# An FFT convolution on one Trainium2 core: the last two frequency slots contracted from copied lanes instead of from a DMA gather

## Chip, cores and metric

One core of a Trainium2 chip runs the whole program. The metric is the time of one execution on the device in microseconds (us), a median over runs; a profiled execution gives the trace. Engines are named as the profile names them: PE (TensorE matmul), PEld (its weight load), DVE (VectorE), ACT (ScalarE), POOL (GpSimd), SP (SyncE, which here only issues DMAs).

## What is computed

A 7x7 circular convolution of one 224x224 image with 96 channels in and 96 out, written with FFTs:

```python
wp = jnp.pad(w, ((0, H - K), (0, W - K), (0, 0), (0, 0)))
Xf = rfft2(x, axes=(1, 2)); Wf = rfft2(wp, axes=(0, 1))
Yf = jnp.einsum('bhwi,hwio->bhwo', Xf, Wf)
y = irfft2(Yf, (H, W), axes=(1, 2)).astype(jnp.bfloat16)
```

Inputs and output are bf16, x is 1x224x224x96 and w is 7x7x96x96.

## The kernel before

The kernel doesn't run two-dimensional FFTs. Along the height it cuts the image into 8 blocks of 28 rows (`NJ`, `B`) and takes a short real transform of each, as a matmul with a matrix `Fm`; that gives 17 frequency slots (`NS`) of two parts (real and imaginary; in the first and last slot two real values). Along the width it works in polyphase form with a fast three-term FIR scheme on the taps. The inverse transform along the height is again a matmul, with a matrix `G`.

The width is cut into 7 tiles `t` of 32 pixels; a tile is 16 pixel pairs `w` (`TW`). Work on a tile runs in 17 rounds, one per slot `s` (`b_round`, line 607). A round convolves over the width on PE into two PSUM banks, b0 and b1; between the two halves and behind the second the program calls `mid()` and `end()`, which put other PE work there. ACT multiplies b0 by -0.5 (`tt_`), which DVE's `u` and `v` read beside b0 and b1; their sum (`ysum`, on DVE or POOL) is the round's result `yf`, 128 partitions (16 w by 8 blocks) by 384 (two parts, two phases of a pixel pair, 96 channels). In the last tile, TL = 6, the sums of slots 14, 15 and 16 are on DVE. DVE also builds the planes `J` that PE convolves (`jit`, line 566).

Results are written to DRAM (`scr`) in groups of three slots, read back with partitions turned to (block, slot, part) and contracted by `G`: the jobs of `c_jobs` (line 776), eleven per tile, each two matmuls of 384 columns and two evictions. `CQ[6] = (3, 5)` puts eight jobs into the last tile's rounds; six jobs of tile 5 are left over when it ends. Rounds, jobs and everything else are in an order written out by hand: each engine's instructions are chained in program order (`_Ordered`, line 91), and the DMAs of SP form one queue, those of ACT another. `evac` and `tail_evac` (lines 132 and 142) choose DVE or ACT for each eviction from a running sum of modelled costs; `tail_evac` holds once `tail[0]` is set.

The last tile can't wait for a full round trip, so it is split by `SLAST = (0, 9, 12, 15, 17)`:

- Slots 0 to 8 are written to `scra`, read back in round 11 as `tl_a` (72 rows: 4 blocks x 9 slots x 2 parts, the other 4 blocks beside them), and contracted with `GA`, which holds four copies of `G`'s rows on its diagonal.
- Slots 9 to 11 and 12 to 14 go through `scrb` into 48 rows each of `tl_b` (`load_b`, line 753), the first in round 14, the second behind round 16.
- Slots 15 and 16 are turned on the core: a matmul with a permutation `PT` (`turn_mm`, line 720), a copy to SBUF (`turn_out`, line 725), and for each slot and part one DMA that takes 128 packets of 384 bytes into 8 rows of `tl_b`. Two of the four are issued by SP and two by ACT.
- `GB` (128 rows: 8 blocks x 8 slots x 2 parts) contracts `tl_b`, in two column sets for the two halves of the blocks.

Behind round 16 (lines 1013 to 1031) the six late jobs run, three before the turning matmuls and three after, then the queued output DMAs. The closing stage (lines 1036 to 1062) makes 16 output tiles of 112 x 384: `first` multiplies `tl_a` by `GA` into a PSUM bank, `second` adds `tl_b` by `GB` and evicts. Eight firsts run ahead (eight banks); ten matmuls on a zeroed tile `wu` (`WARM`) stand between them and the seconds, adding nothing to the sums; the other eight firsts are woven in from the fifth second on.

The matrices are made far ahead: `GA`, `GB` and `PT` are zeroed by POOL in round 15 of the first two tiles, which run woven together (lines 938 to 945), and filled by 28 small SP DMAs in tiles 3 and 4 (`g_parts`, line 756). The last tile-5 row group (`LATE`) is loaded in round 5 of tile 6 over filter slots 5 and 6, which are no longer needed then.

Of the kernel before, what the change touches and what calls it, by code (L numbers as in the profile page):

```python
# [14 lines left out]
B = 28  # L15
# [18 lines left out]
PGRP = ((0, 5), (5, 8), (8, 11), (11, 14), (14, 17))  # L34
YGRP = ((0, 3), (3, 6), (6, 9), (9, 12), (12, 15), (15, 17))
YGRPL = ((0, 3), (3, 6), (6, 9), (9, 12), (12, 15), (15, 17))
SLAST = (0, 9, 12, 15, 17)
SA = SLAST[1]
ND = SLAST[-2]
SLOAD = (SA + 2, 14)  # L40
YMAX = 3
YBUF = 4
JGB = ((0, 3), (3, 6), (6, 9), (9, 12), (12, 15), (15, 17))
# [23 lines left out]
def kernel(  # L67
# [92 lines left out]
    KA = 4 * 2 * SA  # L160
    NL = len(SLAST) - 1
    KB = [NJ * 2 * (SLAST[i + 1] - SLAST[i]) for i in range(1, NL)]
    RB = [sum(KB[:i]) for i in range(NL - 1)]
    assert sum(KB) == 128
# [550 lines left out]
    tt_tiles = {}  # L715
    puts = []
    turns = {}
    zt = [WF[:, i].rearrange("p t o -> p (t o)")[:, 0:4 * C] for i in range(NS - ND)]

    def turn_mm(s):  # L720
        pz = bank()[:, 0:4 * C]
        TE.matmul(pz, lhsT=PT[:], rhs=turns[s], start=True, stop=True)
        return pz

    def turn_out(s, pz, copy, eng):
        i, n = s - ND, 2 * (NS - ND)
        copy(out=zt[i], in_=pz)
        for r in range(2):
            p = RB[-1] + 2 * i + r
            eng.dma_start(out=tl_b[p:p + (NJ - 1) * n + 1:n].rearrange("p w e -> p (w e)"), in_=zt[i][:, r * 2 * C:(r + 1) * 2 * C])  # L730

    def load_t(t, gi, h):
        if (t, gi, h) == LATE:
            tt = WF[:, 5:7].rearrange("p s t o -> p (s t o)")[:, 0:8 * 2 * C].rearrange("p (w e) -> p w e", e=2 * C)
# [16 lines left out]
    tl_b = tl_all[:, 2 * TW2:3 * TW2].rearrange("p (w e) -> p w e", e=2 * C)  # L751

    def load_b(i):
        dma(tl_b[RB[i]:RB[i] + KB[i]], scr_tiles[(TL, 1 + i)].rearrange("w j s (r e) -> (j s r) w e", r=2))

    def g_parts():
        for j in range(4):
            dma(GA[j * 2 * SA:(j + 1) * 2 * SA, j * B:(j + 1) * B], G[0:2 * SA, 0:B])
            yield
        for j in range(NJ):  # L760
            for i in range(NL - 1):
                s, s1 = SLAST[i + 1:i + 3]
                n = 2 * (s1 - s)
                dma(GB[RB[i] + j * n:RB[i] + (j + 1) * n, j // 4, j % 4 * B:(j % 4 + 1) * B], G[2 * s:2 * s1, 0:B])
# [11 lines left out]
    def c_jobs(t):  # L776
        jobs = []
        w0 = t * 2 * TW
        for gi, h in LT if t < TL - 1 else LTL:
# [3 lines left out]
            def mk_(q, gi=gi, h=h, nq=nq, hold=hold):  # L783
                def put(j0, nj, px, npx, row, col):
                    yo = hold["yo"]

                    def go():
                        dma(out[0, j0 * B:(j0 + nj) * B, w0 + px:w0 + px + npx, :].rearrange("h w c -> h (w c)"),
                            yo[row:row + nj * B, col:col + npx * C])
                    if tail[0] or t == TL - 1 and gi != 2:  # L790
                        outs.append(go)
                    else:
                        go()

                def f():
                    if q % 2 == 0:
                        hold["yo"] = new_yo()
                    tt = tt_tiles[(t, gi, h)]
                    yo = hold["yo"]
                    nj = 2 if q == 2 else 3  # L800
                    for b in range(2):
                        pb = bank()[0:nj * B, 0:4 * C]
                        TE.matmul(pb, lhsT=G[0:nj * FR, 0:nj * B],
                                  rhs=tt[0:nj * FR, 4 * q + 2 * b:4 * q + 2 * b + 2, :].rearrange("p w e -> p (w e)"), start=True, stop=True)
                        k = 2 * (q % 2) + b
                        ev = (yo[0:nj * B, k * 4 * C:(k + 1) * 4 * C], pb, 4 * C)
                        if tail[0] == 2:
                            waiting.append(ev)
                        else:
                            evac(*ev)  # L810
# [17 lines left out]
    LATE = (TL - 1, 1, 1)  # L828
    LTL = ((2, 0), (0, 0), (1, 0), (0, 1), (1, 1))
    outs = []  # L830
    waiting = []
    NTT = 4
    held = [0, 0]
    pend = []
# [67 lines left out]
    for r in range(NS + LAG):  # L902
# [28 lines left out]
        if r == PGRP[-2][1] + 1:  # L931
# [7 lines left out]
            GB = g_pool.tile([128, 2, 4 * B], BF16, name="GB")  # L939
            GE.memset(GA[:], 0.0)  # L940
            GE.memset(GB[:], 0.0)
            PT = g_pool.tile([128, 128], BF16, name="PT")
            GE.memset(PT[:], 0.0)
            pv = PT.rearrange("p (j w) -> p j w", j=NJ)
# [16 lines left out]
    if NP2:  # L961
        ps0_cm.__exit__(None, None, None)
        ps_cms = [tc.tile_pool(name="ps", bufs=NP2, space=bass.MemoryType.PSUM),
                  tc.tile_pool(name="psb", bufs=8 - 2 * NP2, space=bass.MemoryType.PSUM)]
        pools["ps"], pools["psb"] = (c.__enter__() for c in ps_cms)
    cj = c_jobs(0)
    gp = g_parts()
    for t in range(2, NT):
        if t == TL:
            scr_tiles[t] = None  # L970
            scr_tiles[(t, 0)] = dr_pool.tile([TW, NJ, SA, 4 * C], BF16, name="scra")
            for i in range(1, NL - 1):
# [18 lines left out]
        for s in range(NS):  # L991
# [7 lines left out]
                queue_c(t - 1)  # L999
            if t in (3, 4):  # L1000
                next(gp, None)
            if t == TL and s == 5:
                load_t(*LATE)
            if t == TL and s in SLOAD:
                i = SLOAD.index(s)
                if i:
                    load_b(i - 1)
                else:
                    sv = scr_tiles[(TL, 0)].rearrange("w (g j) s (r e) -> (j s r) (w g) e", g=2, r=2)
                    for p0, p1 in ((0, 64), (64, KA)):  # L1010
                        dma(tl_a[p0:p1].rearrange("p w g e -> p (w g) e"), sv[p0:p1])
            b_round(t, s, fills(qs, 2 * s), fills(qs, 2 * s + 1), bool(now) if t < TL else s % 3 == 2 or s >= NS - 3, now)
    tail[0] = 1
    load["v"], load["a"] = 1000.0, 0.0
    cj.pop(0)()
    tail[0] = 2
    for _ in range(2):
        cj.pop(0)()
    tail[0] = 1
    pz = [turn_mm(s) for s in range(ND, NS)]  # L1020
    turn_out(NS - 1, pz[1], SE.copy, SE)
    turn_out(NS - 2, pz[0], VE.tensor_copy, DE)
    load_b(NL - 3)
    load["v"], load["a"] = 0.0, 1500.0
    for ev in waiting:
        evac(*ev)
    while cj:
        cj.pop(0)()
    assert not pend
    for f in outs:  # L1030
        f()
# [63 lines left out]
```

## Time and profile before

| what | value |
|---|---|
| median of three runs | 263.33 us (263.27 to 264.97) |
| profiled execution: time, span | 264.47 us, 262.8 us |
| mean granted PE clock | 0.985 |
| ACT, POOL busy | 197.3 us, 98.4 us |
| DVE's sum of slot 14, start and length | 242.31, 0.97 us |
| write of slots 12 to 14 issued (ACT) | 243.36 us |
| read of slots 12 to 14 issued (SP) | 248.47 us |
| turn DMAs issued: SP, ACT | 245.69 for 1.46 us, 245.99 for 1.96 us |

The span runs from the first to the last instruction; the profiled execution's own time is 1.67 us longer. Times inside the text are microseconds from the start of the span. Because every operation goes through the helper of `_Ordered`, nearly all instructions carry line 101, and they are told apart by engine, operation and tile. In the trace `xf` is also the memory of `tl_a` and `tl_b`, `J` and `yo` are the output buffers of the jobs, `xn` holds u and v of the last tile, and `tt` holds the last output tiles. A number in brackets behind an instruction is the idle time before it and what ended it.

### The profile page before, as it was taken

To read this page: it belongs to the slowest core of one execution; us is meant where nothing else is said; L and a number is where in the kernel's file an instruction comes from. 1 tells how busy PE (TensorE), PEld (TensorE's weight loads), DVE (VectorE), ACT (ScalarE), POOL (GpSimd) and SP (SyncE) were. 2 spreads that over 40 slices of the span, in tenths; PEclk is the share of its full clock that TensorE was granted. 3 is DMA by queue.
4 is the path that set the end of the run, shared out by engine and by line. 5 is a ranking of instruction groups with operands and counts; after the bars stand their busy time and mean duration, and the time that the engine had idled before them with its cause. 6 is when DMAs were issued, how large, how long until landed. Compare 5 with 4: busy or idle time off the path is not lost.

```text
span 262.8 us, 11954 instructions
## 1 busy us (share of the span) xinstructions
PE 252.9 (96%) x5040; PEld 233.1 (89%) x5040; DVE 221.7 (84%) x464; ACT 197.3 (75%) x470; POOL 98.4 (37%) x154
## 2 busy tenths in 40 slices
PE   8998999999999999999999999999999999989893
PEld 3988999999989999989999998999999999979472
DVE  6889898899999889868887888878988799999824
ACT  8889978697745967988988799887988852664423
POOL 7783124464657632232223412333134413225000
PEclk9999999999999999999999999999999999999869
DMA  6994104511111695997976596879958742878866
GB/s 185 270 184 128 47 6 147 166 50 47 47 51 47 197 258 91 289 331 198 273 209 209 143 283 196 207 203 266 285 158 194 251 136 87 213 188 237 201 210 203
DMA packets 46778, 46.58 MB, mean 177 GB/s; under 512 B 35324, under 2 KB 37952, under 8 KB 46724
## 3 DMA queue, kind: packets, MB, share of 16 engines
q1 hardware_dynamic: 45732, 44.24, 60.8%
q10 hardware_dynamic: 992, 1.57, 1.9%
q8 instruction: 39, 0.64, 1.1%
q14 instruction: 15, 0.12, 0.2%
HBM read 24.46 MB, written 21.14 MB: 174 GB/s over the span
## 4 chain that ended last, share of the span: by engine, by line
PE 71%; DVE 11%; DMA 6%; issue 5%; ACT 3%; POOL 2%; SPq 0%; DVEq 0%; POOLq 0%; ACTq 0%
PE pb L101 71%; DVE J L101 4%; DVE WF L101 3%; DMA WF<-in_x_dram 3%; DMA tt<-scr 2%; ACT xf L101 2%; POOL yf L101 2%; DMA wq<-in_w_dram 1%; DVE v L101 1%; DVE u L101 1%; ACT WF L101 1%; PE ps L101 1%; SPq L101 0%; DVE yf L101 0%; DVE tt L101 0%
## 5 line engine op out<-in xcount | busy, mean ns | idle before, releaser
L101 PE MATMUL pb<-WF,J 96*128 96x96 bf16 x2821 | 162.4, 206 | 1.8 <-DVE J L101 0.7
L101 PEld LDWEIGHTS <-J 96*128 96x128 bf16 x2821 | 137.9, 98 | 10.7 <-issue 3.6
L101 POOL TENSOR_TENSOR yf<-v,u 128x384 bf16<-128x384 f32 x70 | 73.0, 1056 | 124.0 <-issue 72.5
L101 ACT CAST xf<-pb 96x408 bf16<-96x408 f32 (+6 forms) x140 | 65.0, 489 | 3.7 <-PE pb L101 1.6
L101 PE MATMUL pb<-WF,xf 96*128 96x96 bf16 x952 | 59.9, 206 | 0.2
L101 DVE TENSOR_TENSOR J<-xf 96x456 bf16<-96x456 bf16 (+3 forms) x85 | 56.3, 701 | 0.0
L101 PEld LDWEIGHTS <-xf 96*128 96x128 bf16 x952 | 47.1, 98 | 1.0 <-PE ps L101 0.6
L101 PE MATMUL pb<-Fm,xn 118*128 118x136 bf16 (+4 forms) x576 | 43.9, 203 | 0.8 <-ACT WF L101 0.6
L101 PE MATMUL pb<-tt,Gm 102*84 102x384 bf16 (+1 forms) x128 | 31.4, 327 | 0.1
L101 ACT CAST yo<-pb 84x384 bf16<-84x384 f32 (+1 forms) x61 | 26.1, 480 | 5.6 <-PE pb L101 3.6
L101 PEld LDWEIGHTS <-xn 118*128 118x128 bf16 x576 | 28.6, 97 | 1.3 <-issue 1.1
L101 ACT CAST J<-pb 84x384 bf16<-84x384 f32 (+1 forms) x63 | 27.3, 490 | 2.1 <-DMA xf<-scrb 2.1
L101 DVE TENSOR_TENSOR J<-J 96x912 bf16<-96x912 bf16 (+2 forms) x42 | 25.3, 603 | 0.0
L101 ACT CAST WF<-pb 96x480 bf16<-96x480 f32 (+1 forms) x43 | 21.5, 556 | 0.9 <-PE pb L101 0.8
L101 PEld LDWEIGHTS <-wq 128*128 128x128 bf16 (+1 forms) x288 | 19.7, 149 | 0.2
L101 PE MATMUL pb<-wq 128*128 128x120 bf16 x192 | 15.2, 224 | 0.0
L101 DVE TENSOR_TENSOR WF<-WF 96x960 bf16<-96x960 bf16 x15 | 14.0, 934 | 1.4 <-ACT WF L101 1.3
L101 POOL TENSOR_TENSOR yf<-xn,xn 128x384 bf16<-128x384 f32 x9 | 8.8, 996 | 14.8 <-issue 12.1
L101 PEld LDWEIGHTS <-Gm 102*84 102x84 bf16 (+1 forms) x132 | 11.3, 117 | 1.6 <-issue 0.6
L101 DVE TENSOR_TENSOR yf<-v,u 128x384 bf16<-128x384 f32 x20 | 11.6, 578 | 0.7
L101 ACT COPY xf<-xf 96x816 bf16<-96x816 bf16 (+4 forms) x18 | 10.8, 652 | 0.0
L101 PEld LDWEIGHTS <-wu 128*128 128x128 bf16 (+1 forms) x33 | 4.8, 151 | 6.0 <-issue 2.9
(404 smaller groups left out, 270.8 us busy)
## 6 DMA issues: line engine op xcount, KB each, us to landing
scr<-yf SPq DMA_DIRECT2D x30, 288.0 KB
xn<-in_x_dram SPq DMA_DIRECT2D x12, 672.0 KB
tt<-scr SPq DMA_DIRECT2D x23, 336.0 KB
out_dram<-yo SPq DMA_DIRECT2D x12, 252.0 KB
out_dram<-J SPq DMA_DIRECT2D x12, 252.0 KB
tt<-scr SPq DMA_DIRECT2D x6, 288.0 KB
wq<-in_w_dram SPq DMA_DIRECT2D x5, 288.0 KB
WF<-in_x_dram SPq DMA_DIRECT2D x2, 672.0 KB
```

Source lines behind the costliest of these rows:

```text
L101: r = fn(*a, **k)
```

## The change

Slots 0 to 14 now all go through DRAM into `tl_a`, in three chunks (9, 3 and 3 slots), each chunk laid out as 4 blocks by slots by parts with the other four blocks beside them: 120 rows, and one pass with a larger `GA` contracts them. `tl_b`, `GB`, `PT` and the turn are gone.

Slots 15 and 16 aren't turned. Their result has (w, block) on its 128 partitions. For each of four pairs k of slot and part, four copies on DVE or ACT move 32 partitions (4 w by 8 blocks) of it to partitions 32k to 32k+31 of a tile `Z`, the four groups of w side by side. A contraction over the 128 partitions of `Z` picks one w and four blocks by its weights: `GZ` holds, for each of the 32 lanes, `G`'s row of the pair k where the lane matches and zero elsewhere. `GZ` is one POOL multiply of a mask `MK` (128x32) and `Gk` (G's rows spread over partitions by a small matmul with `SEL`), both broadcast to 128x32x28. `first` is now two matmuls of 192 columns with `GZ` (one per w), and `second` is the one with `GA`.

The six late jobs move between the last rounds: three behind round 14, one inside round 15, one behind it, one inside round 16 (`LATEJ`). The write of slots 12 to 14 is issued behind the first of them. `LATE` is loaded in round 3, over filter slots 2 and 3. The copies of slot 15 stand behind its round and the job there; those of slot 16 behind round 16, the last four on ACT, the other twelve on DVE. The read of slots 12 to 14 follows.

```diff
-SLAST = (0, 9, 12, 15, 17)
+SLAST = (0, 9, 12, 15)
-ND = SLAST[-2]
+ND = SLAST[-1]
+LATEJ = {29: 3, 30: 1, 31: 1, 32: 1}
...
+    def z_part(s, r, copy):
+        k = 2 * (s - ND) + r
+        for a in range(TW // 4):
+            zone = (k, a)
+            apart("Z", zone, copy(out=Z[k * QZ:(k + 1) * QZ, a], in_=turns[s][a * QZ:(a + 1) * QZ, r * 2 * C:(r + 1) * 2 * C]))
...
+    def load_a(i):
+        dma(tl_a[8 * SLAST[i]:8 * SLAST[i + 1]].rearrange("p w g e -> p (w g) e"),
+            scr_tiles[(TL, i)].rearrange("w (g j) s (r e) -> (j s r) (w g) e", g=2, r=2))
...
+    def g_turned():
+        pg = bank()[:, 0:B]
+        TE.matmul(pg, lhsT=SEL[0:FR], rhs=G[0:FR, 0:B], start=True, stop=True)
+        SE.copy(out=Gk[:], in_=pg)
+        GE.tensor_tensor(out=GZ[:], in0=MK.unsqueeze(2).to_broadcast([128, QZ, B]), in1=Gk.unsqueeze(1).to_broadcast([128, QZ, B]), op=ALU.mult)
...
-            GE.memset(GB[:], 0.0)
-            PT = g_pool.tile([128, 128], BF16, name="PT")
-            GE.memset(PT[:], 0.0)
-            GE.affine_select(out=pv, in_=pv, pattern=[[-1, NJ], [-NJ, TW]], compare_op=ALU.not_equal, fill=1.0, base=0, channel_multiplier=1)
+            GE.memset(MK[:], 0.0)
+            for k in range(NZ):
+                GE.affine_select(out=MK[:], in_=MK[:], pattern=[[-1, QZ]], compare_op=ALU.not_equal, fill=1.0, base=-k * QZ, channel_multiplier=1)
+            GE.memset(SEL[:], 0.0)
+            GE.affine_select(out=pv, in_=pv, pattern=[[-1, NZ], [0, QZ]], compare_op=ALU.not_equal, fill=1.0, base=-2 * ND, channel_multiplier=1)
...
+    g_turned()
     cj = c_jobs(0)
+    def last_jobs(k):
+        def f():
+            if not tail[0]:
+                tail[0] = 1
+                load["v"], load["a"] = 1000.0, 0.0
+            for _ in range(LATEJ.get(k, 0)):
+                cj.pop(0)()
+                if puts:
+                    puts.pop(0)()
+        return f
...
+            mid, end = fills(qs, 2 * s), fills(qs, 2 * s + 1)
+            if t == TL and s >= ND - 1:
+                mid, end = last_jobs(2 * s), lambda: None
+            b_round(t, s, mid, end, bool(now) if t < TL else s % 3 == 2 or s >= NS - 3, now)
+            if t == TL and s >= ND - 1:
+                last_jobs(2 * s + 1)()
+            if t == TL and s >= ND:
+                for r in range(2):
+                    z_part(s, r, SE.copy if s == NS - 1 and r else VE.tensor_copy)
+    load_a(NL - 1)
...
     def first(g, q):
         pc = bank()[0:M4, 0:4 * C]
-        TE.matmul(pc.rearrange("p (w e) -> p w e", w=2), lhsT=GA[:], rhs=tl_a[:, 2 * q:2 * q + 2, g], start=True, stop=False)
+        for i in range(2):
+            w = 2 * q + i
+            TE.matmul(pc[:, i * 2 * C:(i + 1) * 2 * C], lhsT=GZ[:, w % 4 * NJ + 4 * g:w % 4 * NJ + 4 * g + 4].rearrange("p j m -> p (j m)"),
+                      rhs=Z[:, w // 4], start=i == 0, stop=False)
         return pc
     def second(g, q, pc, yo):
-        TE.matmul(pc, lhsT=GB[:, g], rhs=tl_b[:, 2 * q:2 * q + 2, :].rearrange("p w e -> p (w e)"), start=False, stop=True)
+        TE.matmul(pc.rearrange("p (w e) -> p w e", w=2), lhsT=GA[:], rhs=tl_a[:, 2 * q:2 * q + 2, g], start=False, stop=True)
```

More of the change, by code (lines that the diff above doesn't have):

```diff
@@ L159 @@
     G = cpool.tile([3 * FR, 3 * B], BF16, name="Gm")
-    KA = 4 * 2 * SA
     NL = len(SLAST) - 1
-    KB = [NJ * 2 * (SLAST[i + 1] - SLAST[i]) for i in range(1, NL)]
-    RB = [sum(KB[:i]) for i in range(NL - 1)]
-    assert sum(KB) == 128
+    KA = 8 * ND
+    NZ = 2 * (NS - ND)
+    QZ = 128 // NZ
+    assert NZ == 4 and QZ == 4 * NJ
     XW = 2 * TW * C
@@ L717 @@
     turns = {}
[L718 to L730, printed above, removed]
+    def z_part(s, r, copy):
[3 more added lines that the diff above has]
+            apart("Z", zone, copy(out=Z[k * QZ:(k + 1) * QZ, a], in_=turns[s][a * QZ:(a + 1) * QZ, r * 2 * C:(r + 1) * 2 * C]))
     def load_t(t, gi, h):
         if (t, gi, h) == LATE:
-            tt = WF[:, 5:7].rearrange("p s t o -> p (s t o)")[:, 0:8 * 2 * C].rearrange("p (w e) -> p w e", e=2 * C)
+            tt = WF[:, 2:4].rearrange("p s t o -> p (s t o)")[:, 0:8 * 2 * C].rearrange("p (w e) -> p w e", e=2 * C)
         else:
@@ L750 @@
     tl_a = tl_all[0:KA, 0:2 * TW2].rearrange("p (w g e) -> p w g e", g=2, e=2 * C)
-    tl_b = tl_all[:, 2 * TW2:3 * TW2].rearrange("p (w e) -> p w e", e=2 * C)
-    def load_b(i):
-        dma(tl_b[RB[i]:RB[i] + KB[i]], scr_tiles[(TL, 1 + i)].rearrange("w j s (r e) -> (j s r) w e", r=2))
+    Z = tl_all[:, 2 * TW2:2 * TW2 + 8 * C].rearrange("p (a e) -> p a e", e=2 * C)
+    def load_a(i):
+        dma(tl_a[8 * SLAST[i]:8 * SLAST[i + 1]].rearrange("p w g e -> p (w g) e"),
+            scr_tiles[(TL, i)].rearrange("w (g j) s (r e) -> (j s r) (w g) e", g=2, r=2))
     def g_parts():
[L757 to L764, printed above, removed]
-                yield
+        for i in range(NL):
+            s, n = SLAST[i], 2 * (SLAST[i + 1] - SLAST[i])
+            for j in range(4):
+                p = 8 * s + j * n
+                dma(GA[p:p + n, j * B:(j + 1) * B], G[2 * s:2 * s + n, 0:B])
+                yield
+    def g_turned():
[3 more added lines that the diff above has]
+        GE.tensor_tensor(out=GZ[:], in0=MK.unsqueeze(2).to_broadcast([128, QZ, B]), in1=Gk.unsqueeze(1).to_broadcast([128, QZ, B]), op=ALU.mult)
     yo_free = [J_bufs[2][0:4 * B, i * PXC * C:(i + 1) * PXC * C] for i in range(2)]
@@ L806, in f @@
                         ev = (yo[0:nj * B, k * 4 * C:(k + 1) * 4 * C], pb, 4 * C)
[L807 to L810, printed above, removed]
+                        evac(*ev)
                     if q == 1 and gi < 2:
@@ L830 @@
     outs = []
-    waiting = []
     NTT = 4
@@ L938 @@
             GA = g_pool.tile([KA, 4 * B], BF16, name="GA")
-            GB = g_pool.tile([128, 2, 4 * B], BF16, name="GB")
             GE.memset(GA[:], 0.0)
-            GE.memset(GB[:], 0.0)
-            PT = g_pool.tile([128, 128], BF16, name="PT")
-            GE.memset(PT[:], 0.0)
-            pv = PT.rearrange("p (j w) -> p j w", j=NJ)
-            GE.affine_select(out=pv, in_=pv, pattern=[[-1, NJ], [-NJ, TW]], compare_op=ALU.not_equal, fill=1.0, base=0, channel_multiplier=1)
+            GZ = g_pool.tile([128, QZ, B], BF16, name="GZ")
+            Gk = g_pool.tile([128, B], BF16, name="Gk")
+            MK = g_pool.tile([128, QZ], BF16, name="MK")
+            SEL = g_pool.tile([128, 128], BF16, name="SEL")
+            GE.memset(MK[:], 0.0)
+            for k in range(NZ):
+                GE.affine_select(out=MK[:], in_=MK[:], pattern=[[-1, QZ]], compare_op=ALU.not_equal, fill=1.0, base=-k * QZ, channel_multiplier=1)
+            GE.memset(SEL[:], 0.0)
+            pv = SEL.rearrange("p (k q) -> p k q", q=QZ)
+            GE.affine_select(out=pv, in_=pv, pattern=[[-1, NZ], [0, QZ]], compare_op=ALU.not_equal, fill=1.0, base=-2 * ND, channel_multiplier=1)
         if r == 3:
@@ L971 @@
             scr_tiles[(t, 0)] = dr_pool.tile([TW, NJ, SA, 4 * C], BF16, name="scra")
-            for i in range(1, NL - 1):
+            for i in range(1, NL):
                 scr_tiles[(t, i)] = dr_pool.tile([TW, NJ, SLAST[i + 1] - SLAST[i], 4 * C], BF16, name=f"scrb{i}")
@@ L1001 @@
                 next(gp, None)
-            if t == TL and s == 5:
+            if t == TL and s == 3:
                 load_t(*LATE)
             if t == TL and s in SLOAD:
[L1005 to L1028, printed above, removed]
+                load_a(SLOAD.index(s))
+            mid, end = fills(qs, 2 * s), fills(qs, 2 * s + 1)
[8 more added lines that the diff above has]
+    load_a(NL - 1)
+    assert not cj
     assert not pend
```

## The prediction

> **What bounds the kernel now.** I read the page's busy shares first, then the chain that ended last from 220 us on, the timeline of the last 25 us, a table of half-microsecond windows over it, and last the timeline at 80 to 98 us, where the new constants are built.
>
> ```profile
> PE 252.9 (96%) x5040; PEld 233.1 (89%) x5040; DVE 221.7 (84%) x464; ACT 197.3 (75%) x470; POOL 98.4 (37%) x154
> ```
> PE (TensorE) sets the pace: a PE stall anywhere before the tail is paid in full, unless a later wait swallows it. The chain of waits:
>
> ```profile
> 231.68 13.40 PE pb L101 x266
> ...
> 246.05 1.47 DVE J L101 x3
> 247.52 0.47 DVE yo L101
> 247.99 9.53 PE pb L101 x37
> 257.52 0.02 issue
> 257.54 1.05 DVE tt L101 x2
> ```
> In the tail the path runs through DVE's evictions of the late jobs, which free the bank of the first closing matmul, and then for 9.5 us through PE. No DMA stands there. The timeline of those 9.5 us:
>
> ```profile
> 247.98 2.78 PE L101 MATMUL pb<-xf,GA 72*112 72x384 bf16 x8 [1.02 <-DVE yo L101]
> 250.55 3.41 PE L101 MATMUL pb<-wu 128*112 128x384 bf16 x10
> 253.75 1.44 PE L101 MATMUL pb<-xf,GB 128*112 128x384 bf16 x5
> ```
> The ten filler matmuls (wu), not a load, hold the second products until 253.75: DMA packets under 512 bytes, which the last load consists of, thin out at 251.1. Firsts and fillers run at half rate (0.32 us for 384 columns; 0.165 us later), as the windows show (the third last column, before the DMA share and GB/s, is the granted clock):
>
> ```profile
> 247.50:248.00 0.50, 0.02 (x1) 0.05 (x1) 0.50 (x3) 0.00 (x0) 0.00 (x0) 0.86 0.70 92
> 248.00:248.50 0.50, 0.50 (x2) 0.40 (x3) 0.45 (x1) 0.45 (x2) 0.00 (x0) 0.50 0.62 131
> ...
> 254.50:255.00 0.50, 0.50 (x4) 0.37 (x3) 0.47 (x2) 0.36 (x1) 0.00 (x0) 0.81 0.03 12
> ```
> The clock fell at 247.86 (0.86 = 0.72 of that window at 1.0) and rose at 254.69, 6.7 us after PE restarted.
>
> **The tail, part by part.** Removed: two turning matmuls, a DVE copy (0.56) and an ACT copy (0.48), and four DMAs that occupied SP for 1.46 us and ACT for 1.96 us (245.99 to 247.95). Moved: the six late jobs (twelve 384-column products, twelve evictions) from behind round 16 to between rounds 14 and 16. Added: sixteen 32x192 copies into Z, twelve on DVE and four on ACT; and each first product becomes two of 192 columns.
>
> The eviction planner starts at 1000 against 0, with 555 and 480 per eviction: ACT takes numbers 1, 2, 3, 5, 7, 9, 11, DVE takes 4, 6, 8, 10, 12. Start to start, one costs 0.425 on ACT (two in 0.85) and 0.485 on DVE (four in 1.94). I lay the queues out on today's times. Up to slot 14's sum, which DVE ends at 243.28 behind POOL, nothing moves. The write of slots 12 to 14 waits on ACT for this sum, as today (trigger 243.36, 0.33); ACT's evictions 3 and 5 and round 15's multiply queue behind it: 243.70, 244.12, 244.55, the multiply ending at 244.96. PE isn't short: three jobs cost it 1.0 us and it is through round 15 by 244.5.
>
> DVE after 243.28, in order: evictions 4 and 6 to 244.25; a wait for that multiply to 245.0; u 0.27 (243.20 to 243.47 today); eviction 8, 0.485; v 0.57; sum of 15, 0.55; eviction 10, to 247.35; eight Z copies; eviction 12, 0.485; sum of 16, 0.55; four Z copies. ACT does its four Z copies after the sum of 16. Round 16's last job needs the bank that v of 15 frees at 246.3, so PE ends round 16 at about 247.3, ahead of DVE.
>
> No row shows a 32x192 bf16 copy. On DVE the ends are 0.09 (the 128x1 scalar operation, 0.158 long, less the 0.07 by which u's start-to-start is under its length) and 0.27 (the 192-wide u). I take 0.13, nearer the cheap end, since bf16 planes run faster (304 columns in 0.30). On ACT a 96x192 copy lasts 0.37; less the 0.065 that evictions gain in a row, 0.30; I take 0.32, ends 0.27 and 0.37. So: eight copies 1.05, to 248.4; eviction, 248.9; sum, 249.45; DVE's copies to 250.0, ACT's to 250.8. The firsts start at 250.85 instead of 247.98: **+2.9** (ends of the copies alone: 250.3 to 252.2, +2.3 to +4.2).
>
> From there the work is as long as today if the clock behaves as today: sixteen firsts of 192 columns stream what eight of 384 did (2.57), ten fillers 3.2, seconds at 256.6. PE idles from 247.3 to 250.8, longer than the 1.1 us gap behind which it is at half rate now, so the clock is down. When it returns is unsure: 6.7 us after the restart in this tail, about 4.4 us at the kernel's start (19 products of 512 columns in 6.46 us: some ten at 0.43, the rest at 0.216). I take 6.7, the same instructions at the same place; with 4.4 the tail costs +1.95. The Trainium skill (TensorE: Matmul & The Clock Gate, Part 1) puts the return after one busy window of about 3.4 us; both rows here are longer, and by 3.4 the tail would cost about +1.5 as an estimate.
>
> The later extra eight weight loads hide: DVE's eight final evictions at 0.59 (4.74 in all) bound that stage.
>
> Free: the load of slots 12 to 14 (24 rows, not 48). It is issued when its write has landed (248.47), its packets end at 251.1; the use moves to 256.6, a cover of 5 us. Were the cover gone it would cost its lateness. The store of the outputs follows the evictions.
>
> **The constants.** Two things happen on POOL far ahead of the tail. In round 15 POOL now does two memsets (GB, PT) that give way to MK's and SEL's, and four more selects over 128x32 (0.214 for 118x4, 0.35 for 128x128: 0.24 plus a 0.04 gap): 0.125 + 4 x 0.28 - 0.23 = +1.0 us. POOL's next sum moves from 82.50 to 83.5, behind the DVE plane of 83.22. It still ends near 85.0, where u(85.02) waits for it; the sum after it ends at 86.05 and holds DVE's plane of 85.75. I take **+0.2**; ends 0 and +1.0 (all of it reaching PE's start at 85.88).
>
> The masked weights GZ are one POOL multiply of 896 elements. POOL's 384-element sum takes 1.0 us and a 1-element one 0.19, so 2.1 ns each: 0.19 + 1.9 = 2.1 us (2.7 by the 84-element row, 2.8 ns each). It starts behind POOL's sum, at 92.1 us, and ends at 94.2. A DVE sum or difference with two SBUF inputs waits for a running POOL one:
>
> ```profile
> 231.49 1.96 POOL L101 TENSOR_TENSOR yf<-xn,xn 128x384 bf16<-128x384 f32 x2 [3.15 <-issue]
> ...
> 232.85 1.02 DVE L101 TENSOR_TENSOR yf<-xn,xn 128x384 bf16<-128x384 f32 x1
> ```
> POOL ends at 233.45, DVE 0.42 later; alone this sum takes 0.56. The planes that stand at 93.07 (1.40 and 0.62 us) thus start at 94.2, 1.15 late; u and v of the round behind them too, and v frees its bank at 96.89 instead of 95.74. PE's three products at 95.92 are the eighth bank request after that one: stall 0.97, **+1.0** (ends 0, if PE has cover that I miss, and +1.6). POOL itself idles 3.8 us there and costs nothing.
>
> At nothing: one small matmul and ACT's 128x28 copy (ACT idles 1.0 us at 94); 12 small SP DMAs for the weights instead of 28, and the late row load two rounds earlier on SP, between loads that it already waits among; slots 0 to 8 loaded in one DMA, used 13 us later.
>
> **Sum:** 2.9 + 0.2 + 1.0 = +4.1 us. The profiled execution took 264.47 (span 262.8 and 1.67 around it) and would take 268.6; it stands 1.14 above the median of the three runs, 263.33, from which I forecast **267.4**.
>
> **Rivals.** (a) The clock returns early, as at the kernel's start: tail +1.95, the rest as forecast, 266.5; with GZ covered too, 265.5. For it: the 4.4 us of the start. Against it: 6.7 in this very place. By the Trainium skill's rule above (same page and part) it would be 266.0 as an estimate; no row here bears 3.4 us out.
> (b) The other side: PE's clock never falls in the tail, because the moved jobs keep PE active until 247.3. It decides from the point at which the fall at 247.86 is missed and the firsts come before the next one. Then sixteen firsts take 1.4, ten fillers 1.65; from a Z ready at 250.3 the seconds start at 253.35, and at full rate the first eviction comes 0.25 sooner: -0.65, with GZ covered 262.7; with Z copies at half my price and round 15's wait for ACT gone, another -1.5, 261.2. Against it: with PE two thirds busy in the 3.4 us before 247.86, the clock fell all the same.
> (c) The dear ends: tail +4.2, GZ +1.6, selects +1.0: 270.1. For it: copies into one tile may not overlap at all.
> (d) The change leaves the time as it is, because the old turn was on the path and its loss pays for the copies: the chain shows no DMA, and ACT's 1.96 us of issuing ended as the firsts began, so at most 1 us comes back, and Z's chain is longer: 264 to 266, counted with (a).
>
> **How the numbers follow.** Forecast (266.2 to 268.8) 0.47; (a) with (d) 0.25; (b) 0.15; (c) 0.13. A measurement here tells about 1% (2.6 us) from no change. Faster by more: the far third of (b), 0.06. Within: the rest of (b), most of (a) and (d), 0.29. Slower: the forecast, (c) and the rest of (a), 0.65. The range leaves out half of (b) and half of (c): 262.9 to 269.6.
>
> **What would show it.** The first closing matmul 2.9 us later against round 14's sum; the granted clock at 0.5 through firsts and fillers; a POOL operation of 2.1 us at 92 with a plane behind it; DVE busy without a break from 245 to 250. I'm wrong if the copies come at under 0.1, if PE keeps its clock, or if PE shows no gap at 95 to 97 us.

## The result, and the profile after

| | time before | time after | ratio |
|---|---|---|---|
| medians of six runs each | 263.13 us (261.87 to 264.97) | 266.06 us (265.72 to 266.41) | 1.0109 (1.0072 to 1.0146) |
| profiled execution | 264.47 us, span 262.8 us | 265.72 us, span 264.0 us | |

The changed kernel is about 2.9 us slower. The profiled execution of before that the prediction worked from was a high one; a second profiled execution of the unchanged kernel (run e8_before_again below: 263.31 us, span 261.6 us) lies near the median, so both stand in the comparison. Everything is measured from the start of DVE's sum of slot 14, since up to there the two kernels do nearly the same work, the constants and a few DMAs apart.

| distance from the start of slot 14's sum, us | before, shown | before, e8 | after |
|---|---|---|---|
| the sum itself, from the start of the span | 242.31 | 241.85 | 242.01 |
| first closing matmul | 5.67 | 6.13 | 8.19 |
| first second product | 11.44 | 10.75 | 13.35 |
| end of DVE's last eviction | 16.75 | 15.74 | 18.41 |
| from there to the end of the span | 3.74 | 4.01 | 3.58 |

Against e8 the span is 2.4 us longer: 0.29 less up to round 15 of the first tiles, 0.44 more from there to round 14 of the last tile, 2.67 more in the tail, 0.43 less behind the last eviction. The chain that ended last, after the change (start, us, what):

```profile
248.62 0.55 DVE yo L102
249.18 0.03 issue
249.21 0.57 DVE yf L102
249.78 0.02 issue
249.80 0.36 ACT xf L102
250.16 0.04 issue
250.20 9.18 PE pb L102 x56
```
Where the chain of before stepped from a DVE eviction (`yo`) to PE at 247.99, it now steps through the sum of slot 16 and a copy into Z (`xf` is Z's memory). The timeline of the same stretch:

```profile
246.90 1.69 DVE L102 COPY xf<-yf 32x192 bf16<-32x192 bf16 x8
249.80 1.46 ACT L102 COPY xf<-yf 32x192 bf16<-32x192 bf16 x4 [3.11 <-DVE yf L102]
249.80 0.89 DVE L102 COPY xf<-yf 32x192 bf16<-32x192 bf16 x4
250.20 2.73 PE L102 MATMUL pb<-xf,GZ 128*112 128x192 bf16 x16 [3.90 <-ACT xf L102]
252.72 2.80 PE L102 MATMUL pb<-wu 128*112 128x384 bf16 x10
255.36 0.98 PE L102 MATMUL pb<-xf,GA 120*112 120x384 bf16 x5
```
PE stands idle for 3.90 us until the first copies of slot 16 are there. Its sixteen firsts take as long as the eight of before (2.73 against 2.78), the fillers follow, and the seconds are on at full rate. The granted clock (third last column) in two windows:

```profile
247.50:248.00 0.50, 0.00 (x0) 0.00 (x0) 0.46 (x4) 0.00 (x0) 0.00 (x0) 0.94 0.91 168
254.50:255.00 0.50, 0.50 (x4) 0.36 (x3) 0.00 (x0) 0.00 (x0) 0.00 (x0) 0.73 0.18 68
```
0.94 in a window of 0.5 us is 0.44 us at full rate, so the clock fell at 247.94; 0.73 puts its return at 254.77, 4.57 us after PE's restart. Far ahead, the constants show in these rows:

```profile
84.43 0.36 DVE L102 SCALAR_TENSOR_TENSOR u<-pb,tt__2532 128x192 f32<-128x192 f32 x1 [0.93 <-POOL yf L102]
84.84 0.32 PE L102 MATMUL pb<-Fm,xn 118*128 118x72 bf16 x5 [0.18 <-DVE u L102]
...
90.35 0.18 PE L102 MATMUL pb<-Gm,SEL 34*128 34x28 bf16 x1
...
90.58 0.18 ACT L102 CAST Gk<-pb 128x28 bf16<-128x28 f32 x1 [0.34 <-PE pb L102]
...
91.50 1.69 POOL L102 TENSOR_TENSOR GZ<-MK,Gk 128x896 bf16<-128x896 bf16 x1
...
92.55 0.55 DVE L102 TENSOR_TENSOR yf<-tt__2836,pb 128x384 bf16<-128x384 f32 x1 [1.41 <-ACT tt__2836 L102]
...
93.02 1.43 DVE L102 TENSOR_TENSOR J<-xf 96x1824 bf16<-96x1824 bf16 x2
```
The same two DVE rows (92.55 and 93.02) read in e8:

```profile
92.11 0.55 DVE L101 TENSOR_TENSOR yf<-tt__2818,pb 128x384 bf16<-128x384 f32 x1 [0.89 <-ACT tt__2818 L101]
...
92.58 1.40 DVE L101 TENSOR_TENSOR J<-xf 96x1824 bf16<-96x1824 bf16 x2
```
The selects push POOL's sum back; DVE's `u` waits for it and PE for `u`. Behind the first tiles, ACT's copy into Gk waits for the small matmul with SEL, and ACT's later copy, for which DVE's sum at 92.55 waits, comes 0.52 us behind e8 (this execution was 0.08 ahead there), and with it the sum and the planes. The multiply into GZ takes 1.69 us, to 93.19; the DVE work beside it is at most 0.03 longer than in e8. Segment by segment against e8 (from one ACT multiply to the same one later), round 15 of the first tiles loses 0.16 us, the stretch with the small matmul and the multiply 0.24, and the round at 105 us another 0.33, where PE waits 0.27 us for a DVE that is still behind; the last tile takes 0.30 back.

### The profile page after: what moved, and what is told of

Its sections match the earlier page's. It is cut to its first block, busy times and chain, and to the rows that moved or that the text cites. A ratio compares the mean times of both kernels' runs of the same rounds, so it can differ in the third digit from the quotient of the medians.

```text
span 264.0 us, 11986 instructions
## 1 busy us (share of the span) xinstructions
PE 251.5 (95%) x5055; PEld 233.6 (88%) x5055; DVE 221.4 (84%) x472; ACT 199.1 (75%) x477; POOL 101.0 (38%) x159
## 4 chain that ended last, share of the span: by engine, by line
PE 66%; DVE 22%; issue 5%; DMA 3%; ACT 1%; POOL 1%; DVEq 0%; SPq 0%; ACTq 0%
PE pb L102 60%; DVE J L102 8%; PE ps L102 6%; DVE xn L102 4%; DVE yf L102 3%; DMA xn<-in_x_dram 3%; DVE WF L102 3%; DVE v L102 2%; DVE u L102 1%; DMA scrb<-yf 1%; ACT xf L102 1%; POOL yf L102 1%; DVE xf L102 1%; DVE yo L102 0%; DVE tt L102 0%
## 5 line engine op out<-in xcount | busy, mean ns | idle before, releaser
L102 DVE TENSOR_TENSOR J<-xf 96x456 bf16<-96x456 bf16 (+3 forms) x85 | 55.5, 692 | 0.0
L102 ACT CAST yo<-pb 84x384 bf16<-84x384 f32 (+1 forms) x62 | 26.7, 483 | 5.5 <-PE pb L102 4.3
L102 ACT CAST J<-pb 84x384 bf16<-84x384 f32 (+1 forms) x65 | 28.2, 491 | 1.5 <-PE pb L102 1.5
L102 ACT CAST WF<-pb 96x480 bf16<-96x480 f32 x42 | 21.2, 563 | 0.1
```

Of the source, the lines that this page charges most:

```text
L102: r = fn(*a, **k)
```

## The experiments

Two theories stood at first. One: the loss is made in the tail, by the longer way of slots 15 and 16 to the first products, by PE's idle time, the clock behind it, and fillers that still stand between firsts and seconds. The other: it is made by the constants on POOL, 150 us earlier. Later runs ask whether the moved jobs or the copies delay the tail, and what else holds the seconds. A letter in an expectation stands for what that expectation says of it. Ratios are to the kernel before, with their 95% intervals.

### e1_consts_only: the kernel before with the new constants alone

```diff
+            GZ = g_pool.tile([128, QZ, B], BF16, name="GZ")
+            Gk = g_pool.tile([128, B], BF16, name="Gk")
+            MK = g_pool.tile([128, QZ], BF16, name="MK")
+            SEL = g_pool.tile([128, 128], BF16, name="SEL")
...
+    g_turned()
     cj = c_jobs(0)
```
MK, SEL, Gk and GZ are made as in the changed kernel, beside GB and PT, and not used by anything.

> The kernel before, with the new constants (MK, SEL, Gk, GZ) made on top of the old ones and never used; the turn and the tail stay. Theory A (the tail alone costs the 2.9 us): within 0.5 us of before, since the trace of the changed kernel shows PE 0.16 us later behind round 15 and 0.2 us later behind the multiply. Theory B (the constants on POOL cost the forecast 1.2 us): 1.0 to 1.6 us slower than before, with a PE gap at 84 to 86 or at 95 us.

Measured: 265.91 us, ratio 1.0092 (1.0062 to 1.0122). Here POOL does old and new constants, so it is more than the change adds:

```profile
83.01 1.68 POOL L101 TENSOR_SCALAR_AFFINE_SELECT MK<-MK 128x32 bf16<-128x32 bf16 x4
...
86.22 0.36 DVE L101 SCALAR_TENSOR_TENSOR u<-pb,tt__2539 128x192 f32<-128x192 f32 x1 [1.72 <-POOL yf L101]
86.63 0.32 PE L101 MATMUL pb<-Fm,xn 118*128 118x72 bf16 x5 [0.90 <-DVE u L101]
```
Up to round 14 of the last tile this kernel loses 1.12 us against e8, 0.90 of it in the PE stall shown. The constants are paid for in PE's time, as forecast, but 1.12 isn't the 2.4 us of the medians. The span of this execution is 3.1 us longer than e8's: 0.83 of that is lost ahead of the constants, and the rest behind round 14. There the firsts wait 1.89 us for the read of slots 0 to 8, a wait that neither theory has, but they start at +6.45, only 0.32 later than in e8. What costs more is the clock: it is down from 249.51 to 256.34, twice as long as in e8, and the seconds start at +12.22 instead of +10.75. The last runs below take up what else holds the seconds; what the medians owe to the constants alone stays open.

### e2_fillers_ahead: fillers in PE's gap

```diff
-WARM = 10
+WARM = 0
...
+    pf = bank()
+    for _ in range(22):
+        TE.matmul(pf[0:M4, 0:384].rearrange("p (a b) -> p a b", a=3), lhsT=wu[:, 0:M4], rhs=wu[:].unsqueeze(1).to_broadcast([128, 3, 128]),
+                  start=True, stop=True)
     live = {k: first(*k) for k in order[:8]}
```
The changed kernel, with 22 fillers ahead of the firsts and none behind.

> The changed kernel with 22 fillers ahead of the first products instead of 10 behind them, in the 3.9 us in which PE idles. Theory A (the time is lost on PE: an idle PE loses its clock, then firsts and fillers run at half rate on the path): clock at 1.0 through the tail, firsts in 1.4 us instead of 2.5, the second products when the load has landed (252.2 at the latest), about 3 us faster than the changed kernel, at or below before. Theory B (the load of slots 12 to 14 or the constants hold it): the second products start at 255.4 as now, less than 0.5 us gained.

Measured: 264.25 us, ratio 1.0017 (0.998 to 1.0054): level with before.

```profile
246.53 3.75 PE L102 MATMUL pb<-wu 128*112 128x384 bf16 x22
250.59 1.52 PE L102 MATMUL pb<-xf,GZ 128*112 128x192 bf16 x16 [0.31 <-ACT xf L102]
253.91 0.99 PE L102 MATMUL pb<-xf,GA 120*112 120x384 bf16 x5 [1.80 <-DMA xf<-scrb]
```
Z comes no earlier (the firsts start at +8.18 from slot 14's sum, 242.41), but the clock stays at 1.0 until 260.2, the firsts take 1.52 us instead of 2.73, and no filler stands behind them. Then the next wait shows: 1.80 us for the read of slots 12 to 14, which in the changed kernel lay under the fillers. It is the only version of the change whose interval includes the time of before.

### e3_no_fillers: the fillers left out

```diff
-WARM = 10
+WARM = 0
```

> The changed kernel without the ten fillers. Theory A: the second products follow the firsts at about 252.7 instead of 255.4, at half rate until the clock returns about 4.6 us after PE's restart or one 3.4 us window later: 1.2 to 2.3 us faster than the changed kernel. Theory B (the load ends the wait): the gap that the fillers leave stays open until about 255 and nothing is gained.

Measured: 264.92 us, ratio 1.0051 (1.0021 to 1.0082). Its profiled execution, 267.63 us, lies some 2.7 us above its median, so it is read within the tail only:

```profile
253.46 2.73 PE L102 MATMUL pb<-xf,GZ 128*112 128x192 bf16 x16 [3.89 <-ACT xf L102]
255.98 1.81 PE L102 MATMUL pb<-xf,GA 120*112 120x384 bf16 x5
```
PE's gap is the same 3.89 us, the seconds follow at once, and they start at half rate (1.81 us for five against 0.98). So the fillers, which stand behind the gap and no longer fill it, cost the changed kernel some 1.1 us by the medians (266.06 to 264.92; 1.5 by the two ratios). They cost more than the seconds lose at half rate without them; the intervals of the ratios just overlap.

### e4_jobs_behind: the late jobs behind the copies

```diff
-LATEJ = {29: 3, 30: 1, 31: 1, 32: 1}
+LATEJ = {33: 6}
...
-            if t == TL and s >= ND - 1:
-                last_jobs(2 * s + 1)()
             if t == TL and s >= ND:
                 for r in range(2):
                     z_part(s, r, SE.copy if s == NS - 1 and r else VE.tensor_copy)
+            if t == TL and s >= ND - 1:
+                last_jobs(2 * s + 1)()
```
The changed kernel with all six late jobs behind round 16 and its copies.

> The changed kernel with all six late jobs behind round 16 and the copies, as before the change. Theory A (the chain to Z on DVE is what is late: evictions among the last rounds delay u, v, the sums and the copies): Z's first column group is ready about 246.8 instead of 250.2, the firsts then wait for banks of the late jobs, to about 249, 0.5 to 1.5 us faster than the changed kernel. Theory C (the moved jobs save as much as they cost): within 0.5 us, or slower, since twelve evictions then stand between the copies and the firsts.

Measured: 265.41 us, ratio 1.0074 (1.0041 to 1.0106).

```profile
247.15 1.43 ACT L102 COPY xf<-yf 32x192 bf16<-32x192 bf16 x4 [2.84 <-DVE yf L102]
248.60 3.13 ACT L102 CAST J<-pb 84x384 bf16<-84x384 f32 x8
250.52 2.77 PE L102 MATMUL pb<-xf,GZ 128*112 128x192 bf16 x16
```
Slot 16's copies now start at +4.63 from slot 14's sum (242.52) instead of +7.79, but the firsts at +8.00 instead of +8.19: the evictions stand behind the copies, and the firsts need their banks. The order of jobs and copies hardly matters here; both go through DVE and ACT ahead of the firsts, and the interval overlaps that of the changed kernel. What is new among that work are the copies: in the changed kernel 1.69 + 0.89 us on DVE, where the turn had one copy of 0.56. That this is 2.02 more, beside firsts that start 2.06 later than in e8, can be chance: DVE also has three of the late evictions there instead of six, and waits 1.55 us for ACT.

### e5_consts_spread and e6_copies_shared

```diff
+            if t == 4:
+                next(gt, None)
```
In e5 the changed kernel makes MK, SEL and GZ in tile 4, one step in each round, the multiply in four pieces of 224 elements (`gt` is `g_turned` with a `yield` behind each step).

> The changed kernel with the same constants made elsewhere: the memsets, selects, the small matmul and the multiply (in four pieces of 224 elements) one per round in tile 4, where POOL idles some 3 us between sums. Theory B (the constants on POOL in round 15 and behind the first two tiles stall PE): PE gets back the gap of 0.2 us at 84.8, the 0.2 us at 90.4 and the 0.3 us at 105.3, 0.5 to 1.2 us faster than the changed kernel. Theory A (the tail alone): within 0.3 us of it.

Measured: 266.32 us, ratio 1.011 (1.0071 to 1.015): a miss. Round 15 of the first tiles, without old and new selects, takes 0.37 us less than in e8, and the stretch to 105 us runs as there. But the stretch of tile 4 in which the steps now stand takes 1.26 us more than in e8 (61.56 instead of 60.30), 1.06 of it between 163.94 and 168.56. The trace shows what stands there: the small matmul, one step behind the select that makes SEL, holds PE for POOL.

```profile
165.46 0.18 PE L102 MATMUL pb<-Gm,SEL 34*128 34x28 bf16 x1 [0.77 <-POOL SEL L102]
```
Up to round 14 the constants cost 0.57 against 0.44, so in this order of steps they only moved. That they must cost as much wherever they are put is not shown: 0.77 us of it is this one wait.

```diff
-                    z_part(s, r, SE.copy if s == NS - 1 and r else VE.tensor_copy)
+                    z_part(s, r, SE.copy if r else VE.tensor_copy)
```
In e6 ACT makes half of slot 15's copies too.

> The changed kernel with the second half of slot 15's copies on ACT, which idles 3.1 us there, instead of DVE: DVE's eight copies become four. Theory A (DVE's chain to Z sets the start of the firsts, and the rest follows it): the firsts start 0.85 us earlier, fillers and seconds too, 0.6 to 0.9 us faster than the changed kernel, unless the clock returns at the same absolute time, then some 0.4. Theory B: no gain.

Measured: 265.54 us, ratio 1.011 (1.0059 to 1.0162), not to be told from the changed kernel. The firsts come at +7.69 instead of +8.19. DVE is 0.85 us less busy, but ACT's copies (0.365 us each, start to start) now stand ahead of ACT's own copy of round 16's bank, and DVE waits 0.51 us for that.

### e7_combined: several at once

```diff
-SLOAD = (SA + 2, 14)
+SLOAD = (SA + 2,)
...
     load_a(NL - 1)
+    load_a(NL - 2)
```
e5 and e6 together, 18 fillers ahead of the firsts and none behind, and the read of slots 9 to 11 behind that of 12 to 14.

> The changed kernel with the constants spread over tile 4, slot 15's copies shared with ACT, 18 fillers ahead of the firsts instead of 10 behind, and the load of slots 9 to 11 behind that of slots 12 to 14, so that the write of slots 12 to 14 does not compete with it (it took 6.5 us to land with the load beside it). If PE's idle clock, the constants and the load are the three prices: firsts at 249.7 at full rate, seconds at 251 to 252 when the last load has landed, 3.5 to 5 us faster than the changed kernel and 1 to 2.5 us faster than before. If the write lands no earlier, seconds at 253.5 and level with before.

Measured: 267.58 us, ratio 1.0168 (1.0125 to 1.0212): the slowest of all. The write of slots 12 to 14 did land sooner (4.5 us), but two reads now run one behind the other, the seconds wait 2.69 us for them, until 255.47, and behind that wait the clock falls, at 256.08. The reordering of the reads is what the trace shows on the path; what the other three edits give together, this run can't tell.

### e8_before_again: a second profile of the kernel before

No edit.

> The kernel before, unchanged, for a second trace. If the trace of before that was read for the forecast was a slow draw (264.47 against a median of 263.1), its head or its tail is shorter here: round 15 some 0.7 us earlier, as in the changed kernel's trace, or the clock returning less than 6.8 us after PE's restart.

Measured: 263.31 us, span 261.6 us.

```profile
247.98 2.27 PE L101 MATMUL pb<-xf,GA 72*112 72x384 bf16 x8 [1.48 <-DVE yo L101]
250.04 2.72 PE L101 MATMUL pb<-wu 128*112 128x384 bf16 x10
252.60 0.98 PE L101 MATMUL pb<-xf,GB 128*112 128x384 bf16 x5
```
Same kernel, same instructions, same gap ahead of the firsts; but the clock fell at 248.50 and was back at 251.92, so that firsts, fillers and five seconds take 5.6 us, where the execution shown with the prediction, whose clock was down from 247.86 to 254.69, needed 7.2.

### e9_before_jobs_moved: one part of the change alone

```diff
+LATEJ = {29: 3, 30: 1, 31: 1, 32: 1}
...
+            if t == TL and s >= ND - 1:
+                mid, end = last_jobs(2 * s), lambda: None
...
+            if t == TL and s >= ND - 1:
+                last_jobs(2 * s + 1)()
...
-    for _ in range(2):
-        cj.pop(0)()
...
     pz = [turn_mm(s) for s in range(ND, NS)]
```
The kernel before with its late jobs between the last rounds, by the changed kernel's `last_jobs`; none stays behind round 16, and the turn is kept.

> The kernel before with one part of the change alone: the six late jobs between rounds 14 and 16 (and the late row load over slots 2 and 3 in round 3), the turn of slots 15 and 16, the wider GB and the old constants kept. Theory A (what the change costs in the tail is the way of slots 15 and 16 through the sixteen copies, which nothing of PE's covers; moving the jobs alone takes the evictions off the path): the firsts need only slots 0 to 8 and start right behind round 16, at +5.0 to +5.7 us after round 14's sum instead of +5.7 to +6.1, PE has no gap over 1 us, the seconds start when the fillers or the turn's DMAs end, +9.5 to +11; time 262 to 264 us, ratio 0.995 to 1.003. Rival B (the moved jobs are what delays: DVE's evictions between the rounds hold u, v and the sums of 15 and 16, so that the turn starts late and its DMAs end the path): seconds wait for a turn DMA at +12 or later, time 264.5 to 266 us, ratio 1.005 to 1.011, as the changed kernel.

Measured: 266.1 us, ratio 1.0082 (1.0051 to 1.0114). The first theory's time (262 to 264) is refuted, but the rival's reason isn't borne out either. The firsts do start early, at +6.35, as said, and at full rate. The chain of the profiled execution (267.43 us) ends so:

```profile
243.31 7.73 DMA scrb<-yf
...
251.11 3.41 DMA xf<-scrb
254.52 0.09 issue
254.61 6.76 PE pb L102 x22
```
Not evictions and not the turn's DMAs: the write of slots 12 to 14 takes 7.73 us to land, and only then can its read start. PE stands for 2.88 us, the clock falls at 253.87, and the seconds run at half rate until 260.70. So moving the jobs, which brings the end of PE's own work forward, uncovers the DMA round trip. The firsts are hardly late here because they read slots 0 to 8 alone. The sum of slot 16 is late: it starts at +5.24 (247.51), against +2.21 in e8 (244.06), and in the changed kernel, with eight copies ahead of it, at +7.20 (249.21). The firsts of the changed kernel wait for that sum, so the moved jobs and the copies both delay them.

### e10_before_no_fillers, e11_before_five_fillers, e12_five_fillers_again

```diff
-WARM = 10
+WARM = 0
```
(in e10; 5 in e11 and e12), on the kernel before. They test the prediction's reading that its fillers, not a load, hold the seconds.

> The kernel before without its ten filler matmuls. Theory A (the fillers, not a load, hold the seconds, and the clock comes back with them or without them): the seconds start 0.8 to 1.5 us earlier against round 14's sum, at half rate in part, time 262.0 to 262.8 us, ratio 0.995 to 0.998. Rival C (the load of slots 12 to 14 or the turn's DMAs land only shortly before the fillers end): the seconds start at most 0.3 us earlier behind a DMA wait and run longer at half rate, time 263.2 to 264 us, ratio 1.000 to 1.003.

> The kernel before with five fillers instead of ten. Theory A: half of what the kernel without fillers gains, 262.5 to 263.0 us, ratio 0.997 to 0.999. Rival C: no difference, 263.1 to 263.4 us.

Measured: none, 265.31 us, ratio 1.0075 (1.0044 to 1.0107); five, 264.34 us, ratio 1.001 (0.9971 to 1.005). Without fillers the kernel before is slower, by more than either expectation had: PE stops 3.03 us for the read of slots 12 to 14, the wait that rival C names, and the clock is down from 250.47 to 260.71. With five, the twelve times fall apart: five lie between 261.87 and 262.83, one at 263.81, and six from 264.87 to 267.53. So the last run profiled it again.

> The kernel before with five fillers once more, as its twelve times fall into two groups (261.9 to 262.8 us, and 263.8 to 267.5 us). Theory D (the landing of slots 12 to 14, which is not the same from execution to execution, is a second path beside the fillers): an execution of the lower group has that load issued within 6 us of its write's trigger and the seconds start within 10.3 us of round 14's sum, with a wait of under 0.6 us for it; one of the upper group has it issued 6.5 us or more behind the trigger and a wait of over 1.2 us, as the first profile (6.64, 1.66). Rival E (the groups come from the start of the kernel or from round 14's place in time): the wait and the distance to the seconds are alike in both, and round 14's sum stands over 1.5 us elsewhere than 241.92.

Measured: 263.09 us, just above the lower group. The end of the chain in e11 (265.70 us) and then in e12:

```profile
242.97 6.58 DMA scrb<-yf
...
249.61 3.35 DMA xf<-scrb
252.96 0.09 issue
253.05 6.12 PE pb L101 x19
```

```profile
243.40 4.92 DMA scrb<-yf
...
248.39 3.77 DMA xf<-scrb
252.15 0.09 issue
252.24 3.90 PE pb L101 x19
```
Round 14's sum is at 241.92 and 242.36, so the start of the kernel isn't it. The write lands 1.66 us later behind its trigger in e11, and the seconds start at +11.13 against +9.88. The same 19 products then take 6.12 against 3.90 us, because the clock is back at 258.82 in the one and at 253.44 in the other. With the transfer 1.25 us later, the last eviction is 3.45 us later (DVE's ends at 260.70, +18.78, against 257.69, +15.33). How much of that the transfer alone makes is not shown, since the clock also fell earlier in e11, at +6.65 (248.57) against +7.66 (250.02). The wait in e12, 0.64 us, is just over the 0.6 that theory D allows; the rest is as D has it, on one profile of each group. The landing varies from execution to execution: it came at +9.8 and +11.0 here, and ten fillers end at +10.75 (e8) and +11.44 (the execution shown), so in the kernel before it may fall on either side of their end. No profile with ten fillers shows the seconds waiting for it.

## Why the prediction was right

**The bound of the tail: right for the execution shown, too sure for others.** "No DMA stands there" holds for that trace and for e8. But the round trip of slots 12 to 14 ends at +9.8 to +11.0 (e12, e11), and the ten fillers at +10.75 to +11.44. In the changed kernel the read is issued at 248.59; with the 3.35 to 3.77 us that it takes in e9, e11 and e12 it is there at +9.9 to +10.4, and the seconds start at +13.35. So the cover is there, at 3 us instead of the 5 forecast (1.9 by e2, where the same read holds the seconds until +11.50), and the six times of the changed kernel lie within 0.7 us.

**Z's chain: right in place and nearly in size.** Forecast: firsts at +8.54 (250.85 on today's times). Measured: +8.19. Three steps under it were off and cancelled, so that the size came out this near is partly luck. The planner's shares: rounds 14 and 15 add to the running sums behind the reset to 1000, which I left out, so ACT took nine of the twelve evictions and DVE three, not seven and five; that is about 1 us less on DVE, half of it behind `u`, and `u` of round 15 waits 1.55 us for ACT's multiply behind those evictions. The copies: 0.21 us each on DVE start to start (1.69 for eight) where I took 0.13, between my ends of 0.09 and 0.27 but nearer the dear one; 0.365 on ACT for 0.32. And the firsts don't wait for the last copy: they start at 250.20, while ACT's copies end at 251.26, since a first product reads one column group.

**The clock: the term that was mis-sized.** 6.7 us behind PE's restart was taken; 4.57 came. Counted from the fall, not from the restart, it is the same 6.83 us in both (247.86 to 254.69, and 247.94 to 254.77): PE only restarted later within it. So the tail lost 2.52 us at the firsts and got 0.61 back by the seconds, against the trace shown: +1.66 at the last eviction, under the forecast's 2.9 and near the +1.95 of rival (a). Against e8, where the clock came back sooner before the change, the tail costs +2.67. The Trainium skill (TensorE: Matmul & The Clock Gate, Part 1) puts the return after at least one busy window of about 3.4 us. If the windows run on by themselves, one is enough in the trace of after, where PE is idle in two thirds of the first 3.41 us and busy in the second; it was not enough in the trace of before, where PE was idle for 0.12 us of the first and the clock stayed down.

**The constants: the selects right, the multiply wrong in its mechanism.** Selects +0.2 forecast, +0.16 measured, though POOL's next sum came 1.6 us late and not 1.0. The multiply +1.0 forecast; 0.24 + 0.33 was lost in that stretch and at 105 us, but the traces don't show the multiply in it. It takes 1.69 us, not 2.1, and DVE's planes don't wait for its end at 93.19: they start at 93.02 and are 0.03 longer than in e8. What shows is what the forecast put at nothing. The small matmul costs PE 0.21 us at 90.35. ACT's copy into Gk was placed at 94 us, where ACT idles; it runs at 90.58, among copies that DVE waits for, and puts DVE's planes 0.52 us behind. So PE doesn't stop at 95 to 97 us; DVE stays behind until PE waits 0.27 us for it at 105.60:

```profile
105.60 0.76 PE L102 MATMUL pb<-WF,J 96*128 96x96 bf16 x14 [0.27 <-DVE u L102]
```
No run has the whole multiply without the matmul and the copy. But in e5 three of its four pieces (172.30 to 174.86) stand in a stretch, 168.56 to 176.91, that takes 8.35 us as in e8. Something that the forecast doesn't name gave 0.30 us back in the last tile. It isn't the moved row load: e1, which doesn't move it, has the same 20.47 us there instead of 20.78. The cause stays open.

**The sum.** +0.44 for the rounds and +2.67 for the tail stand against +1.2 and +2.9. With 0.29 less at the start and 0.43 less behind the last eviction, which the change has no part in that I could show, that is the 2.4 us of the spans. The forecast for the tail was worked out against the execution shown, against which the tail lost 1.66; that +2.9 lies so near the +2.67 against e8 is luck in part.

**The rivals.** (a) is what the clock did against the shown execution. (b), the clock that never falls, did not happen, but e2 forces it and comes out level with before (1.0017), not at 261.2 to 262.7: the read of slots 12 to 14, which (b) took for free, then holds the seconds for 1.80 us. (c) is refuted: DVE's and ACT's copies into Z both start at 249.80, and the tail lost 2.67 at most instead of 4.2. (d) is not needed: the old turn wasn't on the path in either profile of before.

**What stays open.** The parts do not add up: by the ratios the constants alone cost 0.92%, the moved jobs alone 0.82%, and the whole change 1.09%. The traces suggest how that can be, as any lateness ahead of the tail meets the landing and the clock, but they don't show for each median which of the two it was. The reading of e10 and e9 rests on one profile each, both above their medians.

## What to carry to other kernels

Where a chain of transfers and a chain of engine work end within a microsecond of each other, the profile names only the one that came last in that execution; take the distance of the second from the trace and price the change against both. Moving data by engine copies costs the queues of those engines, ahead of whatever stands behind them in order, even when the DMA it replaces wasn't on the path. When a wait moves, look whether the work that used to fill it (here the fillers) still stands where it helps: moved ahead of the firsts it took back nearly all that the change had cost (1.0109 to 1.0017). And a small operation is not free because its engine idles somewhere: what counts is whether it idles at the place in its order where the operation stands.

## What the runs showed of the hardware

- From fall to return of PE's granted clock, each tail in which both were seen shows a whole multiple of 3.41 us, within 0.02: 3.42 (e6, e8, e12), 6.83 (before, after, e1, e3, e4, e5, e9), 10.24 (e10, e11). Which multiple it is, the busy share doesn't tell: in e12 PE was idle for 0.64 of the 3.42 us and the clock came back, in the execution shown before it idled 0.12 of the first 3.41 and the clock stayed down for as long again.
- The write of 288 KB of slots 12 to 14, the same in all, landed 4.5 to 7.7 us after its trigger (e7 and e9).
- A copy of 32x192 bf16 from SBUF to SBUF took 0.21 us on DVE and 0.365 on ACT, start to start, so twelve of them took 2.58 us of DVE where the turn's DMAs had taken 1.96 of ACT and 1.46 of SP.
- POOL's multiply of 896 bf16 elements with both inputs broadcast took 1.69 us, or 1.67 ns an element above the 0.19 of a one-element operation; its 384-element f32 sum, at 1.00 us, takes 2.1 ns each.
